# One loop over 24 token tiles for windowed attention and the MLP behind it

## The chip, the cores and the metric

The kernel runs on one core of a Trainium2 chip. The core has a matrix engine (PE, with its weight loads shown as PEld), a vector engine (DVE), an activation engine (ACT), a general engine (POOL) and a queue engine (SP), each with an instruction stream of its own that runs in order; they meet at semaphores. The metric is device time in microseconds (us), the median of several executions.

## The reference

Attention with 4 batches, 8 heads, 768 positions and 64 columns a head, then an MLP over the 3072 tokens of 512 columns that the heads make together.

```python
keep = is_global | is_local          # key < 8, or 0 <= query - key < 96
dist = np.where(is_global & ~is_local, float(n_local), np.abs(rel))
scores = scale * q @ k.T - slopes[h] * dist        # -1e9 where not keep
a = softmax(scores);  x = (a @ v) gathered to [3072, 512]
h = x @ w_in                                       # [3072, 1024]
solu = h * softmax(h)
ln = (solu - mean(solu)) / sqrt(var(solu) + 1e-6) * g_ln
out = ln @ w_out                                   # [3072, 512]
```

## The kernel before

There are two stages one after the other. The first loops over 4 batches and 2 groups of 4 heads. It loads q, k and v of a pair of heads on SP's queue, casts q and k on ACT (L165, L167) and v on POOL (L203), and transposes q and k on PE into PSUM (pqQ L175, pqK L177), from where DVE copies them (L182, L183). For the 8 global keys it makes one score tile per group (psg L217, L222) with an exp of its own (eg L228). Per head it makes six score products of a key block with 256 queries (psb L251), one exp over 128x1536 (eb L259), a product with the mask on DVE (L270), 11 products with v and 6 with the global v (psav L284), the division (L300, L306) and a transpose back (pxt L312) into xT (L316), which holds all tokens in SBUF. The score tile has one PSUM buffer.

The second stage loops over 24 tiles of 128 tokens. ffn_in makes eight products into ph (L337), an exp e with row sum on ACT (L345), u = e * ph on DVE (L348), its square on ACT (L353), and turns u by a DMA transpose on SP's queue (uT L356). norm_scale makes the scale rs of six tiles at a time on DVE and POOL (L362 to L375). ffn_out, six tiles later, makes eight products into po (L382), scales it on ACT (osb L387) and stores it. ph has three PSUM buffers, po two. Early in the first stage load_weights folds g_ln and the mean into w_out (pm L130, gw_out_sb L134).

A scheduler orders the instructions of each engine; the code gives only the dependences and the pools.

Of the kernel before, what the change touches and what calls it, by code (L numbers as in the profile page):

```python
# [19 lines left out]
def kernel(  # L20
# [29 lines left out]
    big = ctx.enter_context(tc.tile_pool(name="big", bufs=1))  # L50

    ident = const.tile([P, P], FP16, name="ident")
    nc.gpsimd.memset(ident, 0.0)
    nc.gpsimd.affine_select(
        out=ident, in_=ident, compare_op=ALU.not_equal, fill=1.0,
        base=0, pattern=[[-1, P]], channel_multiplier=1,
    )

    diff_i = const.tile([P, NQB], I32, name="diff_i")
    nc.gpsimd.iota(diff_i, pattern=[[1, NQB]], base=0, channel_multiplier=-1)  # L60
    diff_f = const.tile([P, NQB], FP32, name="diff_f")
    nc.vector.tensor_copy(diff_f, diff_i)
    nc.vector.tensor_scalar_max(out=diff_f, in0=diff_f, scalar1=0.0)
    bmask = const.tile([P, H, NQB], FP16, name="bmask")
    for h in range(H):
        nc.scalar.activation(out=bmask[:, h, :], in_=diff_f, func=AF.Exp,
                             scale=-slopes[h])
    bm_flat = bmask.rearrange("p h f -> p (h f)")
    nc.gpsimd.affine_select(
        out=bm_flat, in_=bm_flat, compare_op=ALU.is_ge, fill=0.0,  # L70
        base=0, pattern=[[0, H], [1, NQB]], channel_multiplier=-1,
    )
    nc.gpsimd.affine_select(
        out=bm_flat, in_=bm_flat, compare_op=ALU.is_ge, fill=0.0,
        base=NL - 1, pattern=[[0, H], [-1, NQB]], channel_multiplier=1,
    )

    gmask = const.tile([P, P], FP16, name="gmask")
    glow = const.tile([P, P], FP16, name="glow")
    nc.gpsimd.memset(glow, 1.0)  # L80
    nc.gpsimd.affine_select(
        out=glow, in_=glow, compare_op=ALU.is_gt, fill=0.0,
        base=0, pattern=[[-1, P]], channel_multiplier=1,
    )
    nc.gpsimd.memset(gmask, 1.0)
    nc.gpsimd.affine_select(
        out=gmask, in_=gmask, compare_op=ALU.is_ge, fill=0.0,
        base=-NL, pattern=[[1, P]], channel_multiplier=-1,
    )
    nc.vector.tensor_add(gmask, gmask, glow)  # L90
    gmaskq = const.tile([P, P], FP16, name="gmaskq")
    nc.gpsimd.memset(gmaskq, 1.0)
    for g in range(4):
        nc.vector.tensor_copy(gmaskq[32 * g : 32 * g + NG], gmask[0:NG])

    gbias4 = const.tile([P, 2], FP32, name="gbias4")
    for gi in range(2):
        for g in range(4):
            nc.vector.memset(
                gbias4[32 * g : 32 * (g + 1), gi : gi + 1],  # L100
                -float(NL) * slopes[4 * gi + g],
            )
# [2 lines left out]
    gw_out_sb = const.tile([P, NFC, D_MODEL], FP16, name="gw_out_sb")

    def load_weights():
        w_out32 = wtmp.tile([P, NFC, D_MODEL], FP32, name="w_out32")
        nc.sync.dma_start(out=w_out32, in_=moe_w_out.rearrange("(j p) c -> p j c", p=P))
        g8 = wtmp.tile([NFC, P], FP32, name="g8")  # L110
        nc.sync.dma_start(out=g8, in_=moe_g_ln.rearrange("(j p) -> j p", p=P))
        nc.gpsimd.dma_start(out=w_in_sb, in_=moe_w_in.rearrange("(j p) f -> p j f", p=P))
        id8 = wtmp.tile([NFC, NFC], FP32, name="id8")
        nc.vector.tensor_copy(id8, ident[0:NFC, 0:NFC])
        meanw = wtmp.tile([P, P], FP32, name="meanw")
        nc.vector.memset(meanw, 1.0 / D_FF)
        pg = apsum.tile([P, NFC], FP32, name="pg", space=bass.MemoryType.PSUM,
                        tag="out", bufs=3)
        nc.tensor.transpose(out=pg, in_=g8, identity=id8)
        g32 = wtmp.tile([P, NFC], FP32, name="g32")  # L120
        nc.vector.tensor_copy(g32, pg)
        for j in range(NFC):
            nc.vector.tensor_scalar_mul(
                out=w_out32[:, j, :], in0=w_out32[:, j, :],
                scalar1=g32[:, j : j + 1],
            )
        pm = apsum.tile([P, D_MODEL], FP32, name="pm", space=bass.MemoryType.PSUM,
                        tag="out", bufs=3)
        for j in range(NFC):
            nc.tensor.matmul(out=pm, lhsT=meanw, rhs=w_out32[:, j, :],  # L130
                             start=(j == 0), stop=(j == NFC - 1))
        pm_b = bass.AP(tensor=pm.tensor, offset=pm.offset,
                       ap=[pm.ap[0], [0, NFC], [1, D_MODEL]])
        nc.vector.tensor_tensor(out=gw_out_sb, in0=w_out32, in1=pm_b,  # L134
                                op=ALU.subtract)

# [298 lines left out]
```

## Time and profile before

| what | value |
|---|---|
| median of 3 runs | 284.87 us (281.86 to 285.61) |
| profiled execution | 286.56 us, span 284.9 us |
| PE busy | 241.1 us, 85% of the span |
| PE weight loads busy | 135.5 us, 48% |
| ACT busy | 146.7 us, 52% |
| DVE busy | 135.8 us, 48% |
| POOL busy | 34.3 us, 12% |
| mean granted PE clock | 0.721 of full speed |

The span runs from the first to the last instruction of the profiled execution. A busy share is a mean over two stages with different work, so each stage is read by itself. PE's busy time counts a matmul from its start to its modelled end; matmuls overlap, so the distance between starts tells what one costs in a row of them.

### The profile page before, as it was taken

The page shows a single profiled execution, that of the slowest core. Times are in us where ns is not written, and L with a number is a line of the kernel's source. Part 1 is how long each engine was busy: PE and PEld are TensorE (multiplying, and loading weights), DVE is VectorE, ACT ScalarE, POOL GpSimd, SP SyncE. Part 2 cuts the span into 40 slices and gives each one's busy share as a digit, 9 for nine tenths or more (in the row PEclk, how much of TensorE's full clock was granted, in tenths as well). Part 3 has the DMA queues.
Part 4 walks back from the last instruction along what each step waited for, and adds up shares of the span by engine and source line. Part 5 has one row for each costly group of instructions (what it writes and reads, how often), then busy time and mean ns, then how long its engine had stood idle before and what let it go on. Part 6 is the DMA issues. An engine that isn't in the chain of part 4 may idle for free.

```text
span 284.9 us, 4203 instructions
## 1 busy us (share of the span) xinstructions
PE 241.1 (85%) x1585; PEld 135.5 (48%) x1585; DVE 135.8 (48%) x291; ACT 146.7 (52%) x201; POOL 34.3 (12%) x100
## 2 busy tenths in 40 slices
PE   0546949899998998997997987969999999999774
PEld 0322437565575656655665654544444444444231
DVE  3345296556656654753753753543643433433400
ACT  2735060365555546336336425306988777777622
POOL 3730111010120121011020100000010010010010
PEclk9999985555555555555555555558999999999978
DMA  8999995671845760970881000002957756666632
GB/s 168 201 306 266 218 188 121 113 147 21 169 97 97 140 149 19 168 159 6 169 163 31 2 0 2 0 0 39 137 121 187 175 135 154 154 132 160 155 120 110
DMA packets 105668, 34.88 MB, mean 122 GB/s; under 512 B 101032, under 2 KB 101040, under 8 KB 105648
## 3 DMA queue, kind: packets, MB, share of 16 engines
q1 hardware_dynamic: 101664, 27.28, 49.2%
q10 hardware_dynamic: 3456, 6.29, 6.4%
q0 software_dynamic: 528, 1.05, 2.0%
q8 instruction: 12, 0.20, 0.3%
q14 instruction: 8, 0.07, 0.1%
HBM read 23.07 MB, written 6.29 MB: 103 GB/s over the span
## 4 chain that ended last, share of the span: by engine, by line
PE 62%; ACT 15%; issue 9%; DVE 7%; SPq 2%; DMA 2%; POOL 1%; POOLq 0%; ACTq 0%
PE psb L251 15%; PE psav L284 10%; PE ph L337 9%; PE pxt L312 8%; PE po L382 7%; ACT eb L259 7%; ACT e L345 4%; PE pqQ L175 3%; PE pm L130 3%; PE pqK L177 3%; PE psg L217 3%; ACT eg L228 2%; DMA qq<-in_q_dram 2%; DVE gw_out_sb L134 2%; DVE u L348 1%
## 5 line engine op out<-in xcount | busy, mean ns | idle before, releaser
L259 ACT ACTIVATE eb<-psb 128x1536 f16<-128x1536 f32 x32 | 46.4, 1450 | 62.4 <-PE psb L251 62.1
L251 PE MATMUL psb<-qTt,kTt 64*128 64x256 f16 x192 | 47.3, 407 | 15.5 <-ACT eb L259 12.7
L348 DVE SCALAR_TENSOR_TENSOR u<-e,ph 128x1024 f16<-128x1024 f16 x24 | 29.3, 1222 | 45.0 <-ACT e L345 45.0
L382 PE MATMUL po<-gw_out_sb,uT 128*128 128x512 f16 x192 | 46.4, 390 | 3.7 <-ACT osb L387 3.7
L337 PE MATMUL ph<-w_in_sb,xT 128*128 128x512 f16 x192 | 46.4, 392 | 0.6 <-DVE xT L316 0.6
L251 PEld LDWEIGHTS <-kTt 64*128 64x128 f16 x192 | 22.9, 129 | 31.1 <-issue 22.2
L270 DVE TENSOR_TENSOR eb<-eb,bmask 128x1536 f16<-128x1536 f16 x32 | 30.4, 949 | 9.9 <-ACT eb L259 9.9
L312 PE MATMUL pxt<-ident,onrm 128*64 128x128 f16 x192 | 27.1, 314 | 6.7 <-DVE onrm L306 6.6
L382 PEld LDWEIGHTS <-uT 128*128 128x128 f16 x192 | 19.2, 100 | 28.0 <-issue 6.6
L337 PEld LDWEIGHTS <-xT 128*128 128x128 f16 x192 | 19.2, 100 | 24.8 <-issue 2.7
L353 ACT ACTIVATE sq<-u 128x1024 f16<-128x1024 f16 x24 | 25.4, 1058 | 10.7 <-DVE u L348 9.9
L345 ACT ACTIVATE e<-ph 128x1024 f16<-128x1024 f32 x24 | 24.3, 1011 | 9.5 <-PE ph L337 9.5
L312 PEld LDWEIGHTS <-onrm 128*64 128x64 f16 x192 | 19.4, 164 | 18.0 <-DVE onrm L306 12.1
L316 DVE COPY xT<-pxt 64x768 f16<-64x768 f16 x32 | 17.6, 549 | 17.4 <-PE pxt L312 17.2
L228 ACT ACTIVATE eg<-psg,gbias 128x768 f16<-128x768 f32 x8 | 7.2, 900 | 35.2 <-PE psg L222 35.2
L284 PE MATMUL psav<-vo,eb 128*128 128x65 f16 x352 | 25.0, 243 | 0.3 <-POOL qTt L181 0.3
L284 PEld LDWEIGHTS <-eb 128*128 128x128 f16 x352 | 20.6, 129 | 8.5 <-issue 4.8
L175 PE MATMUL pqQ<-ident,qq 128*128 128x128 f16 x96 | 16.0, 304 | 8.9 <-ACT qq L165 8.9
L387 ACT ACTIVATE osb<-po,rs 128x512 f32<-128x512 f32 x24 | 16.2, 680 | 10.4 <-PE po L382 6.2
L300 DVE RECIPROCAL rl<-psav 128x6 f32<-128x6 f32 x32 | 6.2, 195 | 28.8 <-PE psav L284 28.8
L203 POOL CAST vo<-v 128x384 f16<-128x384 f32 x32 | 17.3, 547 | 14.8 <-DMA v<-in_v_dram 14.7
L306 DVE TENSOR_TENSOR onrm<-psav,rl 128x384 f16<-128x384 f32 x32 | 17.8, 555 | 0.7
(57 smaller groups left out, 198.7 us busy)
## 6 DMA issues: line engine op xcount, KB each, us to landing
qq<-in_q_dram SPq DMA_DIRECT2D x32, 192.0 KB, 3.9
kk<-in_k_dram SPq DMA_DIRECT2D x32, 192.0 KB, 4.2
v<-in_v_dram SPq DMA_DIRECT2D x32, 192.0 KB, 3.9
out_dram<-osb ACTq DMA_DIRECT2D x24, 256.0 KB, 2.1
w_out<-in_moe_w_out_dram SPq DMA_DIRECT2D x1, 2048.0 KB, 14.5
w_in_sb<-in_moe_w_in_dram POOLq DMA_DIRECT2D x1, 1024.0 KB, 9.8
uT<-u SPq DMA_TRANSPOSE x24, 3.1
g<-in_moe_g_ln_dram SPq DMA_DIRECT2D x1, 4.0 KB
```

Source lines behind the costliest of these rows:

```text
L175: nc.tensor.transpose(out=pqQ[:, a, :], in_=qq16[:, a, :], identity=ident)
L251: nc.tensor.matmul(out=psb[:, cj, :], lhsT=kT[:, ts(cj, P)], rhs=qTp[:, ds(P * cj, NQB)], start=st, stop=not st,)
L259: nc.scalar.activation(out=eb.rearrange("p a f -> p (a f)"), in_=psb.rearrange("p a f -> p (a f)"), func=AF.Exp, scale=inv_sqrt_d,)
L270: nc.vector.tensor_tensor(out=eb.rearrange("p a f -> p (a f)"), in0=eb.rearrange("p a f -> p (a f)"), in1=bm_ap, op=ALU.mult,)
L284: nc.tensor.matmul(out=psav[:, rb, :], lhsT=lhs, rhs=rhs_ap, start=st, stop=last, tile_position=tp,)
L306: nc.vector.tensor_tensor(out=onrm, in0=psav[:, :, 0:D], in1=rl_b, op=ALU.mult)
L312: nc.tensor.transpose(out=pxt[0:D, rb, :], in_=onrm[:, rb, :], identity=ident,)
L337: nc.tensor.matmul(out=ph[:, ds(fh * 512, 512)], lhsT=xT[:, j, ts(tb, P)], rhs=w_in_sb[:, j, ds(fh * 512, 512)], start=(j == 0), stop=(j = ...
L345: nc.scalar.activation(out=e, in_=ph, func=AF.Exp, accum_out=st[0][:, i : i + 1])
L348: nc.vector.scalar_tensor_tensor(out=u, in0=e, scalar=1.0, in1=ph, op0=ALU.mult, op1=ALU.mult, accum_out=st[1][:, i : i + 1],)
L353: nc.scalar.activation(out=sq, in_=u, func=AF.Square, accum_out=st[2][:, i : i + 1])
L382: nc.tensor.matmul(out=po, lhsT=uT[:, c, :], rhs=gw_out_sb[:, c, :], start=(c == 0), stop=(c == NFC - 1),)
```

## The change

The two stages become one loop over t, the tile of 128 tokens, in an order written out by hand. Round t makes the scores, exp, mask and value products of tile t in two halves of four heads, the transpose of x of tile t - 1, ffn_in of tile t - 2, ffn_out of tile t - 4 and the store of tile t - 5. A query tile meets its own key block and the one before it. The 8 global keys and their values are copied by POOL into the first 8 rows of each key block, which the window of 96 doesn't reach from the next query tile, so no products of their own are left for them. Later batches' q and k are loaded as pairs of heads with six neighbouring tokens a partition (load_pair), cast on POOL (cast_pair) and transposed two to one pair a round (fill_pair); v of later batches comes by a casting DMA from POOL (load_v). The statistics run on POOL for two tiles at a time. All PSUM tags (t, s, av, h, o) have one buffer. The weights are folded on ACT, PE and DVE in rounds 2 and 3 (gw_round, gw_centre).

```diff
-    xT = big.tile([P, NCC, N_TOK], FP16, name="xT")
-
-    with tc.tile_pool(name="apsum", bufs=1, space=bass.MemoryType.PSUM) as apsum, \
-         tc.tile_pool(name="asb", bufs=3) as asb, \
...
+    def cast_tile0(a):
+        t = st0.pop(a)
+        qk = sb.tile([P, 2, H, D], FP16, name="qk0")
+        nc.scalar.copy(out=qk.rearrange("p w h d -> p (w h d)"),
+                       in_=t[:, 0:2].rearrange("p w h d -> p (w h d)"))
+        nc.gpsimd.tensor_copy(out=vo[:, 0, a, :, 0:D], in_=t[:, 2])
+        if a == 0:
+            nc.gpsimd.dma_start(out=w_in_sb, in_=moe_w_in.rearrange("(j p) f -> p j f", p=P))
+        if a == 1:
+            nc.gpsimd.dma_start(out=w_out32,
+                                in_=moe_w_out.rearrange("(j p) c -> p j c", p=P))
+            nc.gpsimd.dma_start(out=g_sb, in_=moe_g_ln.rearrange("(j p) -> p j", p=P))
+        return qk
...
+    def load_v(b, a):
+        nc.gpsimd.dma_start(out=vo[:, b, a, :, 0:D],
+                            in_=v[b, :, ts(a, P), :].rearrange("h p d -> p h d"))
+    raws, qkn = {}, {}
+    def load_pair(b, w, pr):
+        t = sb.tile([P, 2, NA * D], FP32, name="raw", bufs=8)
+        nc.sync.dma_start(
+            out=t, in_=(q, k)[w][b, 2 * pr : 2 * pr + 2].rearrange(
+                "m (p a) d -> p m (a d)", a=NA))
+        raws[b, w, pr] = t
+    def cast_pair(b, w, pr):
+        t = sb.tile([P, NA, 2, D], FP16, name="qkn", bufs=4)
+        nc.gpsimd.tensor_copy(
+            out=t.rearrange("p a m d -> p m a d"),
+            in_=raws.pop((b, w, pr)).rearrange("p m (a d) -> p m a d", d=D))
+        qkn[b, w, pr] = t
...
+    with tc.manual_schedule():
+        for a in range(3):
+            load_tile0(a)
...
+        def fill_pair(b, w, pr):
+            if b not in qkT:
+                qkT[b] = sb.tile([P, 2 * NP, S], FP16, name="qkT")
+            pt = psum.tile([P, NA, P], FP16, name="pt", tag="t")
+            src = qkn.pop((b, w, pr))
+            for a in range(NA):
+                nc.tensor.transpose(
+                    out=pt[:, a, :],
+                    in_=src[:, a].rearrange("p m d -> p (m d)"),
+                    identity=ident)
+            nc.vector.tensor_copy(
+                out=qkT[b][:, w * NP + pr, :].rearrange("p (t a) -> p a t", a=NA),
+                in_=pt)
...
+        def scores(n, half):
+            b, a = divmod(n, NA)
+            nb = 2 if a else 1
+            ps = psum.tile([P, 2, 2, 2, P], FP32, name="ps", tag="s")
+            for slot in range(2):
+                pr = 2 * half + slot
+                for blk in range(nb):
...
+                        r = ds(D * m, D)
+                        nc.tensor.matmul(
+                            out=ps[:, m, slot, blk, :],
+                            lhsT=qkT[b][r, NP + pr, ts(a - blk, P)],
+                            rhs=qkT[b][r, pr, ts(a, P)],
+                            start=True, stop=True)
...
+            ebs[n, half] = eb
+            if half == 1 and 1 <= a < NA - 1:
+                nc.gpsimd.tensor_copy(out=qkT[b][:, NP : 2 * NP, ds(a * P, NG)],
+                                      in_=qkT[b][:, NP : 2 * NP, 0:NG])
...
+        def av(n, half):
+            b, a = divmod(n, NA)
+            nb = 2 if a else 1
+            if half == 0:
+                pavs[n] = psum.tile([P, 2, 512], FP32, name="pav", tag="av")
+            pav, eb = pavs[n], ebs.pop((n, half))
+            for i in range(4):
+                m, slot = i % 2, i // 2
+                for blk in range(nb):
...
+                        out=pav[:, half, ds(i * (D + 1), D + 1)],
+                        lhsT=eb[:, m, slot, blk, :],
+                        rhs=vo[:, b, a - blk, 4 * half + i, :],
+                        start=(i == 0 and blk == 0), stop=(i == 3 and blk == nb - 1),
+                        skip_group_check=True)
+            if half == 1 and 1 <= a < NA - 1:
+                nc.gpsimd.tensor_copy(out=vo[0:NG, b, a], in_=vo[0:NG, b, 0])
...
+        def x_transpose(n):
+            x16 = x16s.pop(n).rearrange("p g i d -> p (g i d)")
+            pt = psum.tile([P, NCC, P], FP16, name="pt", tag="t")
+            for c in range(NCC):
+                nc.tensor.transpose(out=pt[:, c, :], in_=x16[:, ts(c, P)], identity=ident)
...
+            ph = psum.tile([P, D_FF], FP32, name="ph", tag="h")
...
+            s0, s1, s2 = sts.pop(n // GT)
+            gp = nc.gpsimd
             t1 = stat.tile([P, GT], FP32, name="t1")
...
+            gp.tensor_tensor(out=rs, in0=t3, in1=nhalf, op=ALU.pow)
+            rss[n // GT] = rs
...
+            po = psum.tile([P, D_MODEL], FP32, name="po", tag="o")
...
+        def gw_round():
+            t = const.tile([P, NFC, D_MODEL], FP16, name="gw_r")
+            for j in range(NFC):
+                nc.scalar.activation(out=t[:, j, :], in_=w_out32[:, j, :],
+                                     func=AF.Copy, scale=g_sb[:, j : j + 1])
+            return t
+        def gw_centre(t):
+            pm = psum.tile([P, D_MODEL], FP32, name="pm", tag="o")
+            for j in range(NFC):
+                nc.tensor.matmul(out=pm, lhsT=meanw, rhs=t[:, j, :],
+                                 start=(j == 0), stop=(j == NFC - 1))
+            for j in range(NFC):
+                nc.vector.scalar_tensor_tensor(
+                    out=gw_sb[:, j, :], in0=w_out32[:, j, :], scalar=g_sb[:, j : j + 1],
+                    in1=pm, op0=ALU.mult, op1=ALU.subtract)
...
+        FILLS = [(NA * b + x, (b + 1, f % 2, f // 2)) for b in range(B - 1)
+                 for f, x in enumerate((0, 0, 1, 2, 3, 3, 4, 5) if b else
+                                       (2, 3, 3, 4, 4, 5, 5, 5))]
+        fill_tile(0)
+        for t in range(NT + LAG + 1):
+            b, a = divmod(t, NA)
+            for tf, what in FILLS:
+                if (tf - 4 if tf >= NA else 1 + (tf > 3)) == t:
+                    load_pair(*what)
+            casts = [what for tf, what in FILLS if (tf - 1 if tf >= NA else tf) == t]
+            if has(t):
+                scores(t, 0)
+            if has(t - 1):
+                av(t - 1, 1)
+                norm(t - 1)
+            if t >= 3 and t + 4 < NT:
+                for n in ((NA, t + 4) if t == 3 else (t + 4,)):
+                    load_v(*divmod(n, NA))
+            if casts and b:
+                cast_pair(*casts.pop(0))
+            if has(t):
+                if b == 0 and a + 1 < NA:
+                    fill_tile(a + 1)
+                mask_mul(t, 0)
+            if has(t - LAG - 1):
+                store(t - LAG - 1)
+            if has(t - 2):
+                ffn_in(t - 2)
+            if has(t - 1):
+                x_transpose(t - 1)
+            if has(t - 2):
+                ffn_exp(t - 2)
+            if has(t):
+                scores(t, 1)
+            if has(t - 2):
+                ffn_u(t - 2)
+            if has(t):
+                mask_mul(t, 1)
+                av(t, 0)
+            if has(t - 2):
+                ffn_sq(t - 2)
+            for what in casts:
+                cast_pair(*what)
+            if t == 2:
+                gwr = gw_round()
+            if t == 3:
+                gw_centre(gwr)
+            if has(t - LAG):
+                ffn_out(t - LAG)
+            for tf, what in FILLS:
+                if tf == t:
+                    fill_pair(*what)
...
-        for n in range(NT + GT):
-            if n < NT:
-                if n % GT == 0:
-                    st = [stat.tile([P, GT], FP32, name=f"s{m}") for m in range(3)]
-                ffn_in(n, st)
-                if n % GT == GT - 1:
-                    rss[n // GT] = norm_scale(st)
-            if n >= GT:
-                ffn_out(n - GT)
```

On PE in the attention stage of before, score products, transposes and value products of several heads follow one another (psb scores, pxt transpose of a head's output, psav value products, vg the global values, pqQ transpose of q):

```order
L251 MATMUL psb<-qTt,kTt 128x256
...
L312 MATMUL pxt<-ident,onrm 64x128
...
L284 MATMUL psav<-vo_959,eb 128x65
...
L284 MATMUL psav<-vg_921,eg 128x65
...
L175 MATMUL pqQ<-ident,qq_1224 128x128
```

and in a round of the changed kernel on PE (the first row of each run of like products; pav value products, ph and po the MLP products, pt transposes of x and of later q or k, ps scores):

```order
L243 MATMUL pav<-vo,eb_928 128x65
...
L281 MATMUL ph<-w_in_sb,xT 128x512
...
L269 MATMUL pt<-ident,x_1002 128x128
...
L203 MATMUL ps<-qkT 128x128
...
L243 MATMUL pav<-vo,eb_989 128x65
...
L337 MATMUL po<-gw_sb,uT 128x512
...
L184 MATMUL pt<-ident,qkn 128x128
```

The eight-product runs ph and po now stand among the attention products, and the vg rows are gone.

On ACT in the attention stage of before, exps of heads (eb) alternate with the casts of q and k:

```order
L228 ACTIVATE eg<-psg,gbias_95 128x768
L165 CAST qq_1183<-qq_1177 128x768
L259 ACTIVATE eb<-psb 128x1536
L167 CAST kk_1184<-kk_1178 128x768
L259 ACTIVATE eb<-psb 128x1536 x2
```

and in a round of the changed kernel on ACT:

```order
L211 ACTIVATE eb_989<-ps 128x1024
L343 ACTIVATE osb<-po,rs 128x512
L345 DMA out_dram<-osb 128x512
L292 ACTIVATE e,s_1027<-ph 128x1024
L211 ACTIVATE eb_1041<-ps 128x1024
L309 ACTIVATE sq,s_1029<-u 128x1024
```

The MLP's exp, square and output copy have moved between the two exps of a tile, and the casts have left.

On POOL in the attention stage of before there are only memsets and the casts of v:

```order
L202 MEMSET vo_1214 128x6
L203 CAST vo_1208<-v_1206 128x6x64
L181 MEMSET qTt 128x128
L203 CAST vo_1214<-v_1212 128x6x64
L202 MEMSET vo_1249 128x6
```

and in the changed kernel, over some one and a half rounds (qkT copy of the global keys, vo copy of the global values, t and rs the statistics, qkn the cast of a pair):

```order
L105 CAST qkn<-raw 128x2x6x64
L221 COPY qkT<-qkT 128x4x8
L317 TENSOR_TENSOR t_1158<-s_1028 128x2
...
L328 TENSOR_TENSOR rs<-t_1160,nhalf 128x2
L250 COPY vo<-vo 8x520
L91 DMA vo<-in_v_dram 128x8x64
L105 CAST qkn<-raw 128x2x6x64
L221 COPY qkT<-qkT 128x4x8
```

The copies that the next scores and value products read now stand in one row behind statistics, casts and DMA issues.

## Rows read from the trace of the kernel before

**Rows 1.** The page's granted PE clock in 40 equal slices, tenths of full speed.

```profile
PEclk9999985555555555555555555558999999999978
```

**Rows 2.** Busy time by stretch: us, engines busy (instructions), PE clock, DMA share, GB/s.

```profile
60.00:140.00 80.00, 74.35 (x617) 48.63 (x616) 47.00 (x103) 38.61 (x36) 11.34 (x40) 0.50 0.60 117
210.00:260.00 50.00, 50.00 (x233) 22.64 (x232) 18.28 (x36) 39.73 (x72) 2.92 (x3) 1.00 0.63 155
```

**Rows 3.** The same view around a fall and the rise of the clock.

```profile
40.00:41.00 1.00, 0.00 (x0) 0.00 (x0) 1.00 (x3) 1.00 (x2) 0.00 (x0) 0.85 0.60 130
194.00:195.00 1.00, 1.00 (x5) 0.44 (x4) 0.00 (x0) 0.99 (x2) 0.00 (x0) 0.85 0.00 0
266.00:268.00 2.00, 0.89 (x6) 0.31 (x4) 0.83 (x1) 1.72 (x5) 0.00 (x0) 1.00 0.70 136
```

**Rows 4.** The chain that ended last: start us, us, what.

```profile
17.63 1.45 PE psb L251 x6
...
52.64 1.45 PE psb L251 x6
...
88.58 0.78 PE pxt L312 x6
...
106.70 1.16 PE psav L284 x17
...
190.26 14.24 PE ph L337 x56
...
211.40 1.73 PE po L382 x8
```

**Rows 5.** Timeline of PE: start us, us, operation.

```profile
35.81 0.51 PE L284 MATMUL psav<-vo,eb 128*128 128x65 f16 x11
...
36.53 0.50 PE L251 MATMUL psb<-qTt,kTt 64*128 64x256 f16 x3
36.96 0.23 PE L175 MATMUL pqQ<-ident,qq 128*128 128x128 f16 x1
...
37.59 0.22 PE L177 MATMUL pqK<-ident,kk 128*128 128x128 f16 x1
```

**Rows 6.** Groups of instructions: busy us, mean ns, idle before.

```profile
L259 ACT ACTIVATE eb<-psb 128x1536 f16<-128x1536 f32 x32 | 46.4, 1450 | 62.4 <-PE psb L251 62.1
L270 DVE TENSOR_TENSOR eb<-eb,bmask 128x1536 f16<-128x1536 f16 x32 | 30.4, 949 | 9.9 <-ACT eb L259 9.9
L348 DVE SCALAR_TENSOR_TENSOR u<-e,ph 128x1024 f16<-128x1024 f16 x24 | 29.3, 1222 | 45.0 <-ACT e L345 45.0
L306 DVE TENSOR_TENSOR onrm<-psav,rl 128x384 f16<-128x384 f32 x32 | 17.8, 555 | 0.7
L316 DVE COPY xT<-pxt 64x768 f16<-64x768 f16 x32 | 17.6, 549 | 17.4 <-PE pxt L312 17.2
L203 POOL CAST vo<-v 128x384 f16<-128x384 f32 x32 | 17.3, 547 | 14.8 <-DMA v<-in_v_dram 14.7
L387 ACT ACTIVATE osb<-po,rs 128x512 f32<-128x512 f32 x24 | 16.2, 680 | 10.4 <-PE po L382 6.2 <-POOL rs L375 4.2
L375 POOL TENSOR_TENSOR rs<-t,nhalf 128x6 f32<-128x6 f32 x4 | 5.3, 1333 | 76.2 <-DVE t L373 76.2
```

**Rows 7.** Timeline of POOL, then of DVE, from 100 us.

```profile
100.46 0.51 POOL L203 CAST vo<-v 128x384 f16<-128x384 f32 x1
...
102.67 1.06 POOL L203 CAST vo<-v 128x384 f16<-128x384 f32 x1
...
102.41 0.96 DVE L270 TENSOR_TENSOR eb<-eb,bmask 128x1536 f16<-128x1536 f16 x1
103.28 0.19 DVE L300 RECIPROCAL rl<-psav 128x6 f32<-128x6 f32 x1
```

**Rows 8.** Timeline of ACT at the start and the end.

```profile
6.73 0.83 ACT L165 CAST qq<-qq 128x768 f16<-128x768 f32 x1
...
281.04 0.69 ACT L387 ACTIVATE osb<-po,rs 128x512 f32<-128x512 f32 x1 [1.04 <-PE po L382]
```

More of the change, by code (lines that the diff above doesn't have):

```diff
@@ L14 @@
 ALU = mybir.AluOpType
+PSUM = bass.MemoryType.PSUM
 P = 128
@@ L43 @@
     NT = N_TOK // P
-    LNSC = 1024.0
+    NP = H // 2
+    GT = 2
+    LAG = 4
+    assert NG <= P - NL + 1
     slopes = [float(2.0 ** (-8.0 * (h + 1) / H)) for h in range(H)]
     inv_sqrt_d = 1.0 / math.sqrt(D)
+    FAR = 65536.0
     const = ctx.enter_context(tc.tile_pool(name="const", bufs=1))
[L50 to L102, printed above, removed]
-    w_in_sb = const.tile([P, NCC, D_FF], FP16, name="w_in_sb")
[L105 to L135, printed above, removed]
@@ L321 @@
[L321 to L334 removed]
+    psum = ctx.enter_context(tc.tile_pool(name="psum", bufs=1, space=PSUM))
@@ new lines, with load_tile0 @@
+    sb = ctx.enter_context(tc.tile_pool(name="sb", bufs=2))
+    stat = ctx.enter_context(tc.tile_pool(name="stat", bufs=4))
+    vo = const.tile([P, B, NA, H, D + 1], FP16, name="vo")
+    w_in_sb = const.tile([P, NCC, D_FF], FP16, name="w_in_sb")
+    w_out32 = const.tile([P, NFC, D_MODEL], FP32, name="w_out32")
+    g_sb = const.tile([P, NFC], FP32, name="g_sb")
+    gw_sb = const.tile([P, NFC, D_MODEL], FP16, name="gw_sb")
+    st0 = {}
+    def load_tile0(a):
+        t = sb.tile([P, 3, H, D], FP32, name="st0", bufs=3)
+        for w, src in enumerate((q, k, v)):
+            nc.sync.dma_start(out=t[:, w],
+                              in_=src[0, :, ts(a, P), :].rearrange("h p d -> p h d"))
+        st0[a] = t
@@ L378, in ffn_out @@
-        def ffn_out(tb):
-            uT = uTs.pop(tb)
-            po = mpsum.tile([P, D_MODEL], FP32, name="po", space=bass.MemoryType.PSUM)
-            for c in range(NFC):
-                nc.tensor.matmul(
-                    out=po, lhsT=uT[:, c, :], rhs=gw_out_sb[:, c, :],
-                    start=(c == 0), stop=(c == NFC - 1),
-                )
-            osb = msb.tile([P, D_MODEL], FP32, name="osb")
-            nc.scalar.activation(out=osb, in_=po, func=AF.Copy,
-                                 scale=rss[tb // GT][:, tb % GT : tb % GT + 1])
-            nc.scalar.dma_start(out=out[ts(tb, P), :], in_=osb)
@@ L391, with ffn_exp @@
-        for n in range(NT + GT):
-            if n < NT:
-                if n % GT == 0:
-                    st = [stat.tile([P, GT], FP32, name=f"s{m}") for m in range(3)]
-                ffn_in(n, st)
-                if n % GT == GT - 1:
-                    rss[n // GT] = norm_scale(st)
-            if n >= GT:
-                ffn_out(n - GT)
+                        start=(j == 0), stop=(j == NCC - 1))
+            phs[n] = ph
+        def ffn_exp(n):
+            if n % GT == 0:
+                sts[n // GT] = [stat.tile([P, GT], FP32, name=f"s{m}") for m in range(3)]
+            i = n % GT
+            es[n] = sb.tile([P, D_FF], FP16, name="e")
+            nc.scalar.activation(out=es[n], in_=phs[n], func=AF.Exp,
+                                 accum_out=sts[n // GT][0][:, i : i + 1])
@@ new lines, with ffn_out, store @@
+        pos = {}
+        def ffn_out(n):
+            uT = uTs.pop(n)
+            po = psum.tile([P, D_MODEL], FP32, name="po", tag="o")
+            for c in range(NFC):
+                nc.tensor.matmul(out=po, lhsT=uT[:, c, :], rhs=gw_sb[:, c, :],
+                                 start=(c == 0), stop=(c == NFC - 1))
+            pos[n] = po
+        def store(n):
+            osb = sb.tile([P, D_MODEL], FP32, name="osb", bufs=3)
+            nc.scalar.activation(out=osb, in_=pos.pop(n), func=AF.Copy,
+                                 scale=rss[n // GT][:, n % GT : n % GT + 1])
+            nc.scalar.dma_start(out=out[ts(n, P), :], in_=osb)
```

334 lines of the change are left out of this document (121 added, 213 removed).

## The prediction, made before the changed kernel ran

> **What bounds the kernel now.** I read the page's clock line first, then busy time by stretch, then the chain of waits, then the durations. There are two stages. From 60 to 140 us PE is busy 74.35 of 80 us at a granted clock of 0.50 (1.2 GHz), while ACT is busy 38.6 and DVE 47.0; from 210 to 260 us PE is busy 50 of 50 us at 1.00 (2.4 GHz), ACT 39.7, DVE 18.3 [rows 2]. So PE is the bound of both, and the first, from about 41 to 190 us, runs it at half speed [rows 1]. The nines of the first slices of that line are no evidence of a fast clock: six 64x256 score products take 1.45 us at 17.6 us as they do at 52.6 us, deep in the slow stretch [rows 4].
>
> What moves the clock? PE had been idle since 37.8 us when it fell between 40 and 41 us; it rose between 194 and 195 us, with PE in unbroken 128x512 products since 190.26 us; and it stayed at 1.00 through 266 to 268 us, where PE worked 0.89 of 2 us [rows 3 to 5]. In the attention stage PE was 93% busy with score products on 64 rows, 65-column products and transposes, and it never rose.
>
> **The change: PE's round.** One round of the new loop handles one tile of 128 tokens; 24 of them carry attention. On PE a round holds 16 products of 128x512 (two MLP products of eight), 16 score products of 128 columns, 16 attention products of 65 columns, four transposes of x and, on average over batches 0 to 2, eight transposes of q and k. Each has a row at both clock levels.
> At 2.4 GHz: eight 128x512 products take 1.73 us [rows 4], so two groups 3.46. Three 256-column score products take 36.96 - 36.53 = 0.43 us, 0.143 each [rows 5]; a 128-column one lies between half of it (0.072) and the same less 128 columns (0.143 - 0.053 = 0.09), so 16 take 1.15 to 1.44; I take 1.3. The 17 attention products from 35.81 to 36.53 us take 0.042 each, so 16 take 0.68. Transposes start (37.59 - 36.96) / 11 = 0.057 us apart [rows 5], so 12 take 0.68. Sum **6.1 us** (5.9 to 6.3).
> At 1.2 GHz: 512 columns are 0.427 us, so 6.83 for 16; scores 1.45 / 12 to that plus 0.014, so 1.93 to 2.16; attention 1.16 / 17 = 0.068, so 1.09; transposes 0.78 / 6 = 0.13, so 1.56 [rows 4]. Sum **11.5 us**.
> Dropped from PE: the global-key scores (psg), and per head six products with vg; they ride in the key block now.
>
> **Does another engine take over?** ACT: the two exps of 128x1024 cost 2 x 1450 x 1024 / 1536 ns = 1.94 us [rows 6]; exp, square and output copy of the MLP cost 39.73 us over the 50 / 3.46 = 14.5 tiles of that stretch, 2.74 each [rows 2]. Sum 4.7. The casts of q and k leave ACT after batch 0. DVE: two mask products 2 x 949 x 2/3 = 1.27, reciprocal 0.19 [rows 7], scaling 555 x 512 / 384 = 0.74, x copy about 0.4 (549 ns for 768 columns), u 1.22, q/k copies 1.33 x 0.55 = 0.73 (up to 1.2 if the strided output costs; no row shows one) [rows 6]. Sum 4.6 to 5.1. DMA: 60% share moved 117 GB/s, so 786 KB of q, k, v per tile cost 786 / 195 = 4.0 us of all engines, and out plus transpose of uT 0.63 x 3.46 = 2.2 [rows 2]; 6.2 us if the 1,536-byte pieces of q and k gain nothing, less if they do. So DMA is level with PE at worst, and idle of loads in the last rounds. On SP each uT transpose waits for u, and the loads of later pairs queue behind it; they are issued four rounds before their transposes on PE, so nobody waits for them.
> POOL: 1.33 casts of 128x768, each twice 547 ns, 1.46; the 8x520 copy 0.74; the issue of a v load about 1 (an estimate, from nothing nearer than a v cast's 0.55); the key copy 0.2; half of eight small statistics, with the pow's 1.33 as upper end [rows 6], 1.2. Sum 4.6. Rows 7 show what can lengthen it: a v cast takes 0.51 us alone and 1.06 when it starts inside DVE's mask product. [...]
>
> **Do the single buffers serialise the round?** Every PSUM tag has one buffer, so I laid one round out from score start 0 at 2.4 GHz. scores half 0 to 0.65; attention half 1 of the tile before to 1.0; ffn_in to 2.7; x transposes to 2.95; scores half 1 to 3.6; attention half 0 to 3.95; ffn_out to 5.7; fill to 6.1. ACT: exp 0.85 to 1.85, store to 2.5, MLP exp 2.9 to 3.9, exp 3.9 to 4.9, square 5.3 to 6.3, just ahead of the next round's exp at 6.95. DVE: norm 1.2 to 2.1, mask 2.1 to 2.75, x copy 3.15 to 3.55, u 4.0 to 5.3, mask to 5.95, fill copy 6.3 to 6.9. Each PE step finds its operand done (scores half 1 needs the exp of 1.85 at 2.95; attention half 1 needs the mask of 5.95 at 6.75; ffn_in needs u of 5.3 at 7.1). So PE bounds the round, with 0.7 us to spare at the tightest. Two rounds in six fill two pairs through the one pt buffer: the second waits for the copy, 0.34 + 0.2 + 0.55 + 0.1 = 1.2 us against the 0.34 counted, +0.3 on average. With 0.3 more for POOL's late copies a round is 6.7 us, and 6.1 in the last batch, which fills nothing. 12 x 6.7 + 6 x 6.1 - 2 (three lighter batch starts) = **115 us** for rounds 6 to 23.
>
> **Batch 0** cannot run at that rate. q of before is cast at 6.73 us [rows 8]; now sixteen mask exps stand ahead of that cast on ACT, so I put it at 8.5, transposes, copy and first scores at 12. Then each step waits for the last at the low clock: exp 1.0, cast 1.1, eight transposes 1.04, copy 0.7, mask 0.6, scores 1.1. Rounds 0, 1, 2 come to 5, 8 and 11.5 us (the third holds the first ffn_in, 3.4 us). Behind round 2 ACT rounds the weights, eight times 680 ns = 5.4 us [rows 6], and all exps and the q/k cast of round 3 queue behind it on ACT; in round 3 DVE has eight of half a u, 4.9 us, and pt and the next norm queue behind those. So round 3 is 24.5 us, round 4 11, round 5, with three fills and five POOL casts, 12. Sum **84 us** (72 to 92), against 11.9 MB of needed data, 61 us at the 195 GB/s above, so data is not last there.
>
> **The end.** From the start of round 24: attention, norm, x transpose 2.4; ffn_in waits for u of the tile before, 6.4; exp, u and square to 10; statistics on POOL 2.3; store 0.7; last ffn_out 1.7; store and output, by before's 281.04 to 284.9, 3.9 [rows 8]. With gaps **20 us**.
> Sum: 84 + 115 + 20 = 219 us of span if all bounds fall on the slow side as laid out; batch 0 was laid out wholly at 1.2 GHz with no step overlapped, and I take 6 us back for that, since ffn_in and gw_centre there are the products that raised the clock [rows 4]: 213. Before's profiled run took 286.56 us for a span of 284.9 and the median is 284.87, so span stands for median: **213 us**, 0.75 of before.
>
> **Rivals.** (1) *The clock stays at 1.2 GHz*, the other side. A round is then 11.5 us of PE. For: PE never rose in 150 us of mixed short products. Against: each round has two unbroken runs of eight 128x512 products, the very thing in which it rose, half of PE's time is such products from then on, and a stretch in which PE worked 0.89 of 2 us did not lower it. Price: 92 + 12 x 11.8 + 6 x 10.9 - 3 + 23 = 319 us. It decides from a mean round of (285 - 84 - 20 + 2) / 18 = 10.2 us. (2) *The clock goes to and fro*, since each group of products meets a wait on a single buffer. For: a round has a dozen semaphore waits on PE. Half the rounds slow gives (213 + 319) / 2 = 266 us. [...] (3) *POOL or DMA sets the round*: POOL in order does statistics, casts, the v issue and both global copies, and PE's next scores and attention wait for the copies. [...] (4) *Batch 0 warms up early and short score products overlap*: 72 + 18 x 5.8 + 19 = 195.
>
> **How the numbers follow.** Forecast 0.60, (4) 0.07, (3) 0.17, (2) 0.07, (1) 0.09. The forecast's own range is 200 to 228. The range reaches from 190 to 255, taking in (3) and (4), and leaves out (1) and (2). Faster by over 2% (about what a measurement of this kernel tells from nothing) is all but (1) and a few hundredths of (2) and (3): 0.88; within 2% 0.03; slower 0.09.
>
> **What the profile after would show.** The clock line at 9 from about the fourth round on; PE over 85% busy with the 128x512 products as its largest groups; rounds of 6 to 7 us between outputs; ACT and DVE at 65 to 75% of a round; some 80 us until the seventh tile's scores. Wrong would be a clock line of fives (1, 2), PE waiting on POOL at the attention or score products (3), or ACT waiting in round 2 for w_out, which would lengthen batch 0.

## The result and the profile after

The changed kernel takes 245.15 us (median of 4 runs, 243.96 to 245.42) against 285.07 us before (4 runs): a ratio of 0.861, 95% interval 0.854 to 0.868. The forecast of 213.0 us was 32 us too low; its range of 190 to 255 us holds the time. The profiled execution took 245.42 us for a span of 243.6. Ratios and intervals here and below go by fast runs alone, that is runs within 1.5% of the kernel's fastest; medians are over all runs, which matters only for e15_fold, where four of six runs, the profiled one among them, are slow.

The page of the changed kernel, busy time and three of the lines in 40 slices (a slice is 6.1 us). PEclk answers to [rows 1]:

```profile
PE 159.5 (65%) x1384; PEld 83.2 (34%) x1384; DVE 160.0 (66%) x208; ACT 128.1 (53%) x199; POOL 89.3 (37%) x196
...
PE   0240682461686527598859875988598798989753
...
DVE  0130438269758468789988988899888876765300
...
PEclk9999999596577965979997999799989999999979
```

Busy time of the changed kernel by stretch, as in [rows 2]: batch 0 in two parts, most of the rounds that transpose q and k, and the rest of the loop.

```profile
core 0: us, PE busy (x) PEld busy (x) DVE busy (x) ACT busy (x) POOL busy (x), PEclk, DMA share, GB/s
0.00:40.00 40.00, 14.66 (x142) 9.25 (x142) 11.41 (x21) 17.29 (x33) 11.40 (x30) 1.00 1.09 237
40.00:93.00 53.00, 25.74 (x196) 14.26 (x197) 35.16 (x38) 19.27 (x29) 20.98 (x39) 0.72 0.57 120
93.00:179.00 86.00, 67.52 (x613) 34.58 (x611) 76.81 (x89) 48.94 (x73) 37.12 (x76) 0.90 0.66 120
179.00:225.00 46.00, 41.08 (x404) 21.29 (x401) 33.90 (x58) 35.87 (x56) 17.67 (x45) 1.00 0.53 102
```

From 93 to 179 us DVE is 89% busy, ACT 57%, POOL 43%: DVE is the bound of these rounds, not PE. The groups of instructions tell why (busy us, mean ns; they answer to [rows 6]):

```profile
L188 DVE COPY qkT<-pt 128x768 f16<-128x768 f16 x24 | 65.4, 2723 | 13.7 <-PE pt L184 13.4
L298 DVE SCALAR_TENSOR_TENSOR u<-e,ph 128x1024 f16<-128x1024 f16 x24 | 29.2, 1218 | 10.5 <-ACT e L292 8.6 <-POOL vo L250 1.6
L228 DVE TENSOR_TENSOR eb<-eb,mask 128x1024 f16<-128x1024 f16 x40 | 27.9, 697 | 1.3 <-ACT eb L211 1.2
L262 DVE TENSOR_TENSOR x<-pav,rl 128x512 f16<-128x512 f32 x24 | 16.6, 692 | 1.1
L271 DVE COPY xT<-pt 128x512 f16<-128x512 f16 x24 | 10.2, 423 | 10.7 <-PE pt L269 10.1
```

The copy of transposed q and k, put at 0.55 us, takes 2.72: 24 x 2.17 = 52 us more of DVE. PE's waits from 93 to 180 us (us in total, times, longest):

```profile
PE pt L184 <- DVE qkT L188: 11.3, 4, 2.9
PE pt L269 <- DVE x L262: 7.2, 6, 1.3
```

The first stands where a round fills two pairs through the one pt buffer, as in the timeline below. The second comes from the same copy: in one of the six, the scaling of x stands behind it on DVE (copy at 110.57, reciprocal at 113.02, x at 113.37, PE waits until 114.11). No PE wait listed there ends at POOL or a transfer. And here is what the clock does behind such a wait, in PE's timeline (start, length; in brackets the wait and what ended it) and then in the granted clock (the third number from the right):

```profile
99.75 0.50 PE L184 MATMUL pt<-ident,qkn 128*128 128x128 f16 x6
103.11 0.49 PE L184 MATMUL pt<-ident,qkn 128*128 128x128 f16 x6 [2.86 <-DVE qkT L188]
103.54 0.40 PE L203 MATMUL ps<-qkT 64*128 64x128 f16 x8
103.87 0.37 PE L243 MATMUL pav<-vo,eb 128*128 128x65 f16 x4
104.05 3.52 PE L281 MATMUL ph<-w_in_sb,xT 128*128 128x512 f16 x8
...
108.31 1.89 PE L337 MATMUL po<-gw_sb,uT 128*128 128x512 f16 x8
```

```profile
100.00:103.00 3.00, 0.25 (x5) 0.13 (x3) 2.91 (x2) 1.11 (x2) 0.00 (x0) 1.00 0.62 113
103.00:104.00 1.00, 0.89 (x18) 0.68 (x18) 0.41 (x2) 0.02 (x1) 0.00 (x0) 0.97 0.82 287
104.00:106.00 2.00, 2.00 (x9) 0.77 (x8) 2.00 (x1) 1.58 (x2) 0.00 (x0) 0.50 0.04 15
106.00:108.00 2.00, 2.00 (x16) 0.83 (x14) 1.84 (x5) 0.39 (x1) 0.00 (x0) 0.66 0.34 131
108.00:110.00 2.00, 2.00 (x22) 1.04 (x17) 1.50 (x4) 1.64 (x3) 0.21 (x1) 1.00 0.00 0
...
130.00:131.00 1.00, 1.00 (x4) 0.28 (x3) 0.95 (x4) 0.00 (x0) 0.40 (x1) 0.50 0.68 90
153.00:154.00 1.00, 1.00 (x4) 0.28 (x2) 0.95 (x3) 0.00 (x0) 0.00 (x0) 0.50 0.26 100
177.00:178.00 1.00, 1.00 (x3) 0.15 (x1) 0.95 (x3) 0.00 (x0) 0.69 (x1) 0.50 0.28 28
```

PE stood 2.86 us for the copy, the clock fell to 0.50, and the eight products that came next took 3.52 us instead of 1.89. With the wait came a second loss, here of 1.6 us. The other three waits of this kind (PE resumed at 126.77, 150.39 and 174.07 us) have a stretch at 0.50 behind them too, the last three rows. That the wait is what lowers the clock is argued from these four, not shown; e14_thinrep below has a wait nearly as long with no fall behind it.

Stages, from PE's timelines (the start of the seventh tile's scores, and of the last tile's second attention half; 93.42 and 222.47 us in the changed kernel):

| | predicted | changed kernel | e2_natural | e15_fold |
|---|---|---|---|---|
| batch 0 | 84, less 6 | 93.4 | 82.5 | 70.7 |
| rounds 6 to 23 | 115 | 129.1 | 105.0 | 105.5 |
| end | 20 | 21.1 | 22.2 | 21.0 |
| span | 213 | 243.6 | 209.6 | 197.2 |

### The profile page after: what moved, and what is told of

Read it like the earlier page. It is cut to its first block, busy times and chain, and to the rows that moved or that the text cites. A ratio compares the mean times of both kernels' runs of the same rounds, so it can differ in the third digit from the quotient of the medians.

```text
span 243.6 us, 3661 instructions
## 1 busy us (share of the span) xinstructions
PE 159.5 (65%) x1384; PEld 83.2 (34%) x1384; DVE 160.0 (66%) x208; ACT 128.1 (53%) x199; POOL 89.3 (37%) x196
## 4 chain that ended last, share of the span: by engine, by line
PE 27%; DVE 24%; ACT 7%; issue 3%; POOL 2%; DMA 1%; ACTq 0%; DVEq 0%; POOLq 0%
DVE qkT L188 16%; PE ph L281 9%; PE po L337 8%; DVE u L298 5%; ACT e L292 4%; PE pt L184 3%; PE pav L243 3%; DVE x L262 2%; PE ps L203 2%; PE pt L269 2%; ACT sq L309 2%; DVE eb L228 1%; ACT osb L343 1%; DMA out_dram<-osb 1%; POOL t L326 1%
## 5 line engine op out<-in xcount | busy, mean ns | idle before, releaser
L188 DVE COPY qkT<-pt 128x768 f16<-128x768 f16 x24 | 65.4, 2723 | 13.7 <-PE pt L184 13.4
L211 ACT ACTIVATE eb<-ps 128x1024 f16<-128x1024 f32 x40 | 40.8, 1019 | 36.2 <-PE ps L203 36.1
L281 PE MATMUL ph<-w_in_sb,xT 128*128 128x512 f16 x192 | 58.5, 459 | 0.6 <-DVE u L298 0.6
L337 PE MATMUL po<-gw_sb,uT 128*128 128x512 f16 x192 | 46.9, 388 | 3.5 <-ACT osb L343 3.5
L184 PE MATMUL pt<-ident,qkn 128*128 128x128 f16 x144 | 13.2, 233 | 31.3 <-DVE qkT L188 23.5
L228 DVE TENSOR_TENSOR eb<-eb,mask 128x1024 f16<-128x1024 f16 (+1 forms) x48 | 31.9, 665 | 1.3 <-ACT eb L211 1.2
L309 ACT ACTIVATE sq<-u 128x1024 f16<-128x1024 f16 x24 | 25.4, 1057 | 11.5 <-DVE u L298 11.5
L243 PE MATMUL pav<-vo,eb 128*128 128x65 f16 x352 | 20.5, 200 | 3.9 <-DVE eb L228 2.1
L184 PEld LDWEIGHTS <-qkn 128*128 128x128 f16 x144 | 10.4, 104 | 36.5 <-issue 23.8
L203 PE MATMUL ps<-qkT 64*128 64x128 f16 x352 | 19.8, 234 | 1.4 <-DVE qkT L175 0.8
L105 POOL CAST qkn<-raw 128x768 f16<-128x768 f32 x24 | 19.9, 839 | 2.3 <-issue 2.2
```

The source lines that it names most:

```text
L105: nc.gpsimd.tensor_copy(out=t.rearrange("p a m d -> p m a d"), in_=raws.pop((b, w, pr)).rearrange("p m (a d) -> p m a d", d=D))
L184: nc.tensor.transpose(out=pt[:, a, :], in_=src[:, a].rearrange("p m d -> p (m d)"), identity=ident)
L188: nc.vector.tensor_copy(out=qkT[b][:, w * NP + pr, :].rearrange("p (t a) -> p a t", a=NA), in_=pt)
L203: nc.tensor.matmul(out=ps[:, m, slot, blk, :], lhsT=qkT[b][r, NP + pr, ts(a - blk, P)], rhs=qkT[b][r, pr, ts(a, P)], start=True, stop=True)
L211: nc.scalar.activation(out=eb_f, in_=ps.rearrange("p m s b f -> p (m s b f)"), func=AF.Exp, scale=inv_sqrt_d)
L228: nc.vector.tensor_tensor(out=eb.rearrange(pat), in0=eb.rearrange(pat), in1=mk.rearrange(pat if n % NA else "p m s f -> p (m s f)"), op=AL ...
```

## The experiments

Theory A: the copy's output steps 12 bytes between neighbouring fp16 values, and that write is the price. Theory B, the rival: the single PSUM buffers let the clock swing, whatever the copy costs. All ratios are to the kernel before.

**e1_contig** writes the copy in one run.

```diff
-                out=qkT[b][:, w * NP + pr, :].rearrange("p (t a) -> p a t", a=NA),
-                in_=pt)
+                out=qkT[b][:, w * NP + pr, :],
+                in_=pt.rearrange("p a t -> p (a t)"))
```

> fill_pair's copy writes qkT in one piece instead of every sixth element (tokens of later batches then stand in another order, so the output is not the reference's). Theory A, the strided copy is what the changed kernel lost: one copy falls from 2.72 to about 0.55 us, 24 of them give 52 us of DVE back, 17 of it in batch 0; rounds 6 to 17 fall from 8.2 to about 5.8 us on average, the clock stays at 1.00 from round 6 on, total 195 to 205. Theory B, single PSUM buffers make the clock swing by themselves: the swings of the clock line stay, rounds stay over 7 us, total 225 or more.

211.29 us, 0.737 (0.733 to 0.742).

**e2_natural** has the same copy, and loads q and k in token order (256-byte pieces, two transfers a pair), so that its tokens stand in the reference's order.

```diff
+        for m in range(2):
             nc.sync.dma_start(
-                out=t, in_=...rearrange("m (p a) d -> p m (a d)", a=NA))
+                out=t[:, m]..., in_=...[b, 2 * pr + m].rearrange("(a p) d -> p a d", p=P))
```

> q and k of later batches loaded in pieces of 256 bytes in token order, so the copy is in one piece and the output is the reference's. Theory A: within 3 us of e1_contig. Rival, the transfers become the bound with four times as many short pieces: POOL waits for raw in its casts, 8 us or more above e1_contig.

210.58 us, 0.734 (0.728 to 0.739): the short pieces cost the kernel no time that is measured. They do cost the transfers some: the queue that holds these loads (packets, MB, share of the 16 engines' time) takes a larger share in e2_natural, the second line, than in e1_contig:

```profile
q1 hardware_dynamic: 50592, 20.45, 46.2%
q1 hardware_dynamic: 81696, 20.45, 56.1%
```

The copy of e2_natural, its clock line, PE's waits from 93 to 180 us, and its busy time from 90 to 190 us:

```profile
L189 DVE COPY qkT<-pt 128x768 f16<-128x768 f16 x24 | 13.3, 556 | 10.1 <-PE pt L185 9.8
...
PEclk9999999758856996799999999999999999999958
```

```profile
PE pt L185 <- DVE qkT L189: 2.4, 3, 1.1
PE pav L244 <- POOL vo L251: 2.1, 4, 0.6
PE pav L244 <- DVE eb L229: 0.6, 1, 0.6
```

```profile
90.00:190.00 100.00, 93.82 (x960) 51.78 (x960) 75.33 (x138) 79.63 (x123) 55.05 (x120) 1.00 0.85 146
```

With the same single buffers the clock stands at 1.00 and PE is 94% busy: B falls for the loop, and PE bounds it as forecast.

**e4_read** turns the step round: DVE reads PSUM in steps and writes one run. **e5_act** gives the strided copy to ACT.

```diff
+                out=qkT[b][:, w * NP + pr, :].rearrange("p (t a) -> p t a", a=NA),
+                in_=pt.rearrange("p a t -> p t a"))
```

```diff
-            nc.vector.tensor_copy(
+            nc.scalar.copy(
```

> the copy reads PSUM in steps of 128 elements and writes in one piece. If only strided writes are dear, a copy takes 0.55 to 0.9 us and the total is as e1_contig; if any step of more than one element is dear, a copy stays near 2.7 us and the total near 245.

> the strided copy runs on ACT. ACT worked 4.7 us of a round of 6.7, so a copy of about 0.85 us fits: total 198 to 210. If ACT pays for the strided write as DVE does (2.7 us), ACT becomes the bound at 4.7 + 1.33 x 2.7 = 8.3 us a round: total 250 or more.

e4_read 211.35 us, 0.737 (0.730 to 0.745); e5_act 268.54 us, 0.937 (0.928 to 0.945). The copy in each:

```profile
L188 DVE COPY qkT<-pt 128x768 f16<-128x768 f16 x24 | 22.9, 955 | 10.2 <-PE pt L184 10.1
```

```profile
L188 ACT COPY qkT<-pt 128x768 f16<-128x768 f16 x24 | 65.0, 2710 | 16.9 <-PE pt L184 16.9
```

It is the write to SBUF in steps that costs, on either engine alike (2.72 us on DVE, 2.71 on ACT, against 0.56 for e2_natural's write without steps); a PSUM read in steps costs 0.4 us (0.96 against 0.56), which the loop hides. On ACT the copy stands ahead of the exps, and the kernel is slower still. A is shown, for some 34 of the 245 us; 211 us is above the 195 to 205 that A alone had promised, and e2_natural's remaining fives stand in batch 0 and in the last slice. No run gave pt a second buffer, so how much of the 34 us the one buffer had a part in stays open.

**What holds the clock?** Built on e2_natural, e8_short cuts each 128x512 MLP product in four of 128 columns; e14_thinrep leaves out 13 of the MLP's 16 products and issues each score product five times.

```diff
-                for fh in range(2):
+                for c in range(8):
...
-                        out=ph[:, ds(fh * 512, 512)], lhsT=xT[:, j, :],
...
+                        out=ph[:, ds(c * 128, 128)], lhsT=xT[:, j, :],
...
```

```diff
-                    for m in range(2):
+                    for m in [0, 1] * 5:
...
-            for j in range(NCC):
+            for j in range(1):
...
-            for c in range(NFC):
+            for c in range(1):
```

> Built on e2_natural (210.58 us, clock 1.00 from 100 us on). Each 128x512 MLP product is cut in four of 128 columns: same columns, same result, four times the instructions. Theory K (it is the long products that keep TensorE at 2.4 GHz; short ones never raised it in the kernel before, rows of 93% busy at 0.50): the clock falls to 0.50 in the loop, a round takes some 12 us, 270 to 310 us. Rival W (what counts is that PE works without long idle stretches, whatever the length): the clock stays at 1.00, the 64 products take 0.055 to 0.062 us each, 3.5 to 4.0 us a round against 3.46, so 211 to 222 us.

> Built on e2_natural (210.58 us, clock 1.00 in the loop). The MLP leaves out 13 of its 16 products (the output isn't the reference's), and each 64-row score product is issued five times over, so that PE is as busy: 64 more of 0.041 us for 13 of 0.216 us. Theory K2 (products on all 128 rows hold the clock up, score products don't; the stage of before that was 93% busy with scores, attention and transposes stood at 0.50): the clock falls to 0.50 in the loop, rounds of 8 to 9 us, 250 to 270 us. Rival W (a busy PE holds it, whatever the product): 1.00, rounds of 5.3 to 6.0 us, 200 to 212 us.

e8_short 211.01 us, 0.740 (0.731 to 0.748); e14_thinrep 212.88 us, 0.745 (0.739 to 0.752), just above W's 200 to 212. The loop in each, 100 to 190 and 90 to 200 us:

```profile
100.00:190.00 90.00, 85.08 (x1607) 77.76 (x1604) 67.46 (x123) 71.42 (x109) 50.22 (x107) 1.00 0.92 143
```

```profile
90.00:200.00 110.00, 80.69 (x1790) 60.05 (x1790) 76.25 (x144) 83.91 (x130) 55.62 (x120) 0.98 0.84 139
```

Neither K nor K2 holds: short products keep 1.00, and 64-row score products in place of most MLP products 0.98. So "the very thing in which it rose", the prediction's first argument against rival (1), was the wrong reason for a right outcome. Why the attention stage of before stood at 0.50 while 93% busy [rows 2] stays open.

e14_thinrep also holds the case that speaks against a long wait as the one thing that lowers the clock: PE stands 2.67 us for the copy, and the clock is at 1.00 before and behind it.

```profile
130.38 0.49 PE L185 MATMUL pt<-ident,qkn 128*128 128x128 f16 x6 [2.67 <-DVE qkT L189]
130.81 1.29 PE L204 MATMUL ps<-qkT 64*128 64x128 f16 x40
132.03 0.30 PE L244 MATMUL pav<-vo,eb 128*128 128x65 f16 x4
```

```profile
127.00:130.00 3.00, 0.71 (x11) 0.51 (x10) 2.38 (x4) 2.14 (x5) 3.00 (x5) 1.00 0.87 200
130.00:135.00 5.00, 4.02 (x99) 3.11 (x99) 2.72 (x6) 2.48 (x4) 1.42 (x3) 1.00 1.67 199
```

What sets it apart from the waits of 2.8 to 2.9 us of the changed kernel, no run tells.

**e12_rows** orders the score products by row half.

```diff
+            for m in range(2):
+                r = ds(D * m, D)
                 for slot in range(2):
```

> Built on e2_natural (210.58 us). The score products of a tile go in another order: the four of heads on rows 0 to 63 first, then the four on rows 64 to 127, where neighbours alternated. Theory S (it was the alternation of row halves that let two 64-row products run at once, 0.33 us for eight; the prediction's 0.08 each is the price without it): eight take 0.55 to 0.70 us, a round 0.4 to 0.7 us more, 213 to 224 us, since PE is busy 93% of the loop. Rival (64-row products of 128 columns cost 0.041 us whatever the order): 0.33 us, 210 to 212 us.

211.83 us, 0.742 (0.735 to 0.748). Scores, then attention, in its timeline:

```profile
175.30 0.41 PE L204 MATMUL ps<-qkT 64*128 64x128 f16 x8
175.64 0.42 PE L244 MATMUL pav<-vo,eb 128*128 128x65 f16 x8
```

Eight take 0.34 us (start to start) in this order too; S falls. At 0.031 each in e14_thinrep (40 in 1.22 us) they are faster than 128 columns of an MLP product (eight of 512 in 1.73 us [rows 4], so 0.216 / 4 = 0.054), which speaks for two running at once; no run isolates that. The two orders differ by 0.01 us in eight (0.33 us in the changed kernel, from 103.54 to 103.87, against 0.34).

**Batch 0**, where e2_natural still waits. e6_castfirst puts the POOL casts of pairs at the head of batch 0's rounds; e7_wlate issues the weight loads a tile later; e9_gwpool rounds the weights on POOL instead of ACT.

```diff
-            if casts and b:
-                cast_pair(*casts.pop(0))
+            for what in casts[: 1 if b else len(casts)]:
+                cast_pair(*what)
+            casts = casts[1:] if b else []
```

```diff
-        if a == 0:
+        if a == 1:
             nc.gpsimd.dma_start(out=w_in_sb, ...)
-        if a == 1:
+        if a == 2:
             nc.gpsimd.dma_start(out=w_out32, ...)
```

```diff
-                nc.scalar.activation(out=t[:, j, :], in_=w_out32[:, j, :], func=AF.Copy, ...)
+                nc.gpsimd.tensor_scalar(out=t[:, j, :], in0=w_out32[:, j, :], ..., op0=ALU.mult)
```

> Built on e2_natural (210.58 us). In batch 0 the POOL casts of q/k pairs now stand at the head of their round instead of behind the statistics. Theory A (what is left over 195 us is batch 0, where PE stands for POOL's in-order queue: 75.2 to 79.1 us in the sixth round, 52.2 to 56.0 us in the fourth, of which DVE's weight centring to 57.8 us hides most): the wait of 3.7 us in the sixth round goes, that of the fourth gives 0 to 1.6 us: 205 to 207 us. Rival (batch 0 is paced by its transfers, POOL's wait only fills the time): 209 to 211 us, the wait turns up at a DMA.

> Built on e2_natural (210.58 us). The two MLP weight loads are issued one tile later (w_in behind tile 1's v cast, w_out behind tile 2's). Theory A (tile 2's q and k land at 22.9 us because 4 MB of weights share the DMA engines): tile 2 lands at 14 to 16 us, ACT's 5.6 us wait for it goes, and 3 to 6 us of it reach the end: 205 to 208 us. Rival (the weights are wanted just as early): the third round's first MLP product waits for w_in, or the weight rounding for w_out, and the time stays at 209 to 212 us.

> Built on e2_natural (210.58 us). The eight weight roundings of 0.62 us go from ACT (38.7 to 43.7 us, PE idle) to POOL, which is idle from 41.8 to 50.2 us. Theory A (they stand ahead of the exp and tile 4's cast on ACT): 4 to 5 us less, 205 to 207 us. Rival (POOL takes 0.7 to 0.85 us each, its v issues, casts and copies queue behind, so PE waits as long): 209 to 212 us.

e6_castfirst 204.02 us, 0.717 (0.711 to 0.723): theory A, a little below its 205 to 207. e7_wlate 208.53, 0.728 (0.721 to 0.736): at the edge, its interval meets e2's. e9_gwpool 211.73, 0.743 (0.736 to 0.750): the rival, because a POOL multiply by a column of scalars has another price than its casts,

```profile
36.21 12.38 POOL L352 TENSOR_SCALAR gw_r<-w_out,g_sb 128x512 f16<-128x512 f32 x8
```

1.55 us each, twice what the rival had counted, where ACT needs 0.62 and a POOL cast of that size 0.61; the global copy of v then came 4.3 us late for PE.

**e11_batch0** joins e6 and e7, sets the wide mask exps behind tile 0's cast, and spreads the weight folding in pairs over rounds 3 and 4. **e15_fold** changes only the places of the folding.

```diff
             if t == 3:
-                gw_round(0, 2)
+                gw_round(0, 6)
             if t == 4:
-                gw_centre(2, 4)
+                gw_centre(4, 6)
...
+            if t == 3:
+                gw_centre(0, 4)
```

> Built on e6_castfirst (204.02 us). Three more moves in batch 0: weight loads one tile later (as e7_wlate), the 128x256 mask exps behind tile 0's cast, and the weight folding spread: two of its eight ACT and DVE steps at a time among the steps of rounds 3 and 4 (before: all eight in one piece, 38.7 to 43.7 us on ACT with PE idle 6.9 us, and 52.6 to 57.9 us on DVE with PE idle 5.6 us in e6_castfirst). Theory A (batch 0 is a chain of in-order waits, each of which can be taken out): 2 us of e7, 1.5 us of the masks, 4 to 9 us of the folding, so 192 to 198 us. Rival T (transfers now set batch 0: 11.9 MB at 195 to 215 GB/s is 55 to 61 us before round 6, and the waits reappear at loads): 200 to 204 us.

> Built on e11_batch0 (204.88 us), whose spread folding only moved the wait: PE stood 3.4 us for the last roundings on ACT (43.7 to 49.8 us) and 4.2 us for the last weight block on DVE (60.8 to 65.0 us), and ran from 49 to 68 us at 0.50 to 0.67. Here six of the eight roundings stand right behind the fifth tile's cast, where ACT had idled 3.3 us, the other two behind the MLP exp; half of the centring stands behind round 3's pair copies, the rest ahead of u. Theory A (the waits, not the transfers, set batch 0): 3 to 7 us less, 198 to 202 us. Rival T (with these waits gone the same time is lost at loads of tiles and pairs): 204 to 206 us.

e11_batch0 204.88 us, 0.717 (0.713 to 0.721): no gain on e6, and outside both forecasts; its moves on the masks and the folding were not run by themselves. e15_fold 198.88 us (195.57 to 199.55, 6 runs), 0.694 (0.687 to 0.700), as theory A had it and the fastest here; each of its six runs is below each of e11_batch0's six (204.30 to 205.51). PE's waits of e11 for the folding (0 to 95 us), and those left in e15 (0 to 90 us):

```profile
PE po L333 <- DVE gw_sb L360: 4.2, 1, 4.2
PE pm L354 <- ACT gw_r L348: 3.4, 6, 1.3
```

```profile
PE pt L167 <- ACT qk L79: 12.6, 5, 6.1
PE pt L167 <- POOL vo L81: 6.9, 1, 6.9
PE pt L180 <- DVE qkT L184: 4.0, 5, 1.0
PE pt L180 <- POOL qkn L106: 2.9, 1, 2.9
PE po L333 <- DMA uT<-u: 2.5, 1, 2.5
```

Both folding waits are gone, and with them 6 us: waits, not transfers, set that part of batch 0. Ahead of some 35 us it is otherwise: two of the waits left, of 6.1 us until 27.41 and of 2.9 us until 35.00, end at casts that had themselves stood for a load.

```profile
26.32 1.04 ACT L79 CAST qk<-st 128x1024 f16<-128x1024 f32 x1 [4.63 <-DMA st<-in_k_dram]
33.96 0.98 POOL L106 CAST qkn<-raw 128x768 f16<-128x768 f32 x1 [11.91 <-DMA raw<-in_q_dram]
```

## Why the prediction was right, and where its size was off

- **What was right** is the direction and the clock it hung on: 0.50 in the attention stage of before [rows 2], 0.90 from 93 to 179 us and 1.00 from 179 to 225 us in the changed kernel. The reason given for it did not hold (e8_short, e14_thinrep), and why the clock stays up is not shown. No run separates what the clock gave from what the products gave that are gone. The traces give the clock as a granted share alone, and no run gives a frequency: the prediction's 1.2 and 2.4 GHz stand for 0.50 and 1.00, at which nine 512-column products of before take 4.02 us (from 190.26 us) and eight take 1.89 (from 211.24 us).
- **That the range holds the time is luck** as to the mechanism. 245 us lies outside the forecast's own 200 to 228; the range reaches it only because it took in rival (3), where POOL or DMA sets the round, and it was DVE that set it (89% busy from 93 to 179 us).
- **The mis-sized step** is "q/k copies 1.33 x 0.55 = 0.73 (up to 1.2 if the strided output costs; no row shows one)". A copy measured 2.72 us (3.5 ns a column, against 0.72 of e2_natural's), 3.6 a round, so by the prediction's other terms DVE's round was 7.5 us instead of 4.6 to 5.1, above PE's 6.1, a case no rival had; rounds 6 to 17 took 7.9 us on average. The wait for the second pair's copy in the one pt buffer, counted at 1.2 us, grew to 2.8 us with it. The upper end of the term was a guess, tied to no row; the doubt was right, its bound not. With the step mended (e2_natural) the kernel takes 210.6 us, 2.4 from the forecast.
- **PE's round** of 6.1 us was too dear: eight score products take 0.33 us, not 0.65. Rounds 6 to 23 of e2_natural are 10 us below the 115 for that (18 x 0.64 = 11.5), rival (4)'s mechanism.
- **Batch 0** was laid out at 84 us, less 6 for a clock that warms early, and came to 82.5 without the dear copy, 4.5 above the 78. The clock did stand above the 0.50 of the layout there (0.74 on average from 40 to 83 us of e2_natural, PE's idle time included), yet the 6 us were not gained. That e2_natural lands so near the forecast is luck in part: 10 us too much for the rounds stand against 4.5 too little for batch 0 and 2.2 for the end.
- **Single buffers** do not serialise the round, as laid out (e2_natural, 94% busy). **Rival (2)** came in part, with a clock of 0.90 from 93 to 179 us. With the same single buffers and waits of 1.1 us at most e2_natural shows no swing from 90 to 190 us; the falls in the changed kernel stand behind waits of 2.8 to 2.9 us.
- **Rival (3)**: no run shows DVE holding POOL up so far that POOL sets the round. POOL was busy 43% from 93 to 179 us of the changed kernel; it made PE wait 8 us in batch 0 of e2_natural (three casts behind statistics), but set no round in the loop.
- **The end**, 20 us forecast, is 21.1.
- Of the signs named for the profile after, these failed: the nines from the fourth round (unbroken only from 179 us), PE over 85% busy (65%), rounds of 6 to 7 us (7.9 in rounds 6 to 17, 5.7 after them), ACT and DVE at 65 to 75% of a round (57 and 89%), and some 80 us until the seventh tile's scores (93.4).
